# A retention layer and a gated feed-forward on one core: slot 5 transposed by DMA, two slots loaded by the hardware queue, a new order

## The chip, the cores and the metric

The kernel runs on one core of a Trainium2 chip. Its engines are TensorE (PE, its weight loads shown apart as PEld), VectorE (DVE), ScalarE (ACT), GpSimd (POOL) and SyncE (SP), which work through their own instruction queues and wait for each other by semaphores. Sixteen DMA engines move data; a transfer is issued either by POOL (in software) or by SP (in hardware). The metric is the device time of one execution in microseconds, the median of several runs.

## The reference

Inputs are q, k and v of shape (4, 8, 768, 64) (batch, head, time, head width), w_in (512, 2048) and w_out (2048, 512), all float32. What is computed:

```python
gamma = 1.0 - 2.0 ** (-5.0 - np.arange(H))
scale = 1.0 / np.sqrt(D)
for t in range(S):
    state = gamma * state + einsum('bhd,bhe->bhde', k[:, :, t], v[:, :, t])
    y[:, :, t] = scale * einsum('bhd,bhde->bhe', q[:, :, t], state)
x = y.transpose(0, 2, 1, 3).reshape(B * S, H * D)      # 3072 tokens of 512
h = x @ w_in
g = h * cos(h)
return g @ w_out
```

## The kernel before

**Slots.** Time is cut into six chunks of 128, batches are taken in two pairs, and one chunk of one pair is a slot: twelve slots, in the order 0, 6, 1, 2, 3, 4, 5, 7, ... of `ORDER`. In a slot the recurrence becomes matrix products: scores k times q, masked to the past, times v, plus q times the state of earlier chunks. q is multiplied by a rising power of gamma and k or v by a falling one ("conversions", `conv_q`, `conv_k`, `conv_v`, to bfloat16). q and k must also be transposed, so that the head width lies on the partitions.

**Transposes.** Slots 0 to 5 are transposed on TensorE against an identity (`t_mm`, L364), into a PSUM bank that ACT or DVE copies to `qkt` (`t_copy`). From slot `DMA_T` = 6 on, SP issues a DMA transpose of the converted q and one of k (`dma_t`, L353).

**Blocks.** The products of a slot with 64-row operands, its scores (L392), masked products (L483), state products (L497, L511), are put out in an order for the four quarters of TensorE's array (`y_block`, `quarters`). From slot 4 on a slot's block also holds the scores of the next slot. `second(p, x, b, u)` says which half of the chunk's keys counts as the later one: a product of the later half needs only 64 of 128 columns. In slots from `SWAP` = 8 on, the halves of k and v are loaded in swapped order for half of the heads and batches, so that the two column halves of the array have as many columns each; below that one has 128 and the other 64.

**Feed-forward.** Two slots are a group of 512 tokens. The first product (`f_mm`, L593; `h_mm`, L614, for the half group of one slot) has 16 blocks of w_in; ACT takes the cosine (L601), DVE multiplies (L605, L622), and the second product (`o_mm`, L638) has four rows of tokens times four quarters of w_out. ACT copies a row out and SP stores it.

**The order of the work.** All up to slot 5's block, groups 0 and 1, and the second product of group 0 is laid out by a planner when the program is written: `Plan` holds operations with engines, a cost, what they come after and a rank. `run` walks through time and gives every free engine the ready operation of the lowest rank; then they are written in the order of their starts, so each engine's queue is fixed. `SHIFT` adds to ranks by name and `ON` fixes an engine. For transfers `Plan.run` keeps one time `self.dma`, at which the transfers so far are through; `rate` and `lag` say how long one takes. What follows is a plain loop (groups 2 to 6), in which first and second products alternate and blocks, conversions, transposes (`conv`) and loads (`load(nc.sync, ...)`) stand at fixed places.

**Loads.** Five buffers each hold q, k and v as loaded (`PRE`). The first q is loaded by SP. All else in the planned part comes through POOL, in the order of `LOADS`: q, k, v of the slots, w_in in pieces, w_out in quarters o0 to o3, last v5, q6, k6, v6, q7, k7, v7. A load of 512 KB in POOL's queue holds POOL for some 1.2 us. Slot 8 is loaded by SP (`l8`, with "ks" and "vs": swapped halves, six DMAs each) after slot 7's transposes; later slots in the loop. The transposes of slots 6 and 7 wait for k7 (`ld["k", 7, 0]`).

**Names of the operations** that the text uses: q6, k6, v6 are loads; cq, ck, cv with slot and batch are conversions; t50, t51 slot 5's transposes on TensorE, eq and ek the copies; dt60 and dt61 the DMA transposes of q and k of slot 6; m the masks.

Of the kernel before, what the change touches and what calls it, by code (L numbers as in the profile page):

```python
# [28 lines left out]
class Plan:  # L29
# [16 lines left out]
    def add(self, engines, cost, fn, after=(), rank=0.0, take=(), give=(), mode=None,  # L46
            spare=0, mb=0.0, rate=0.0, lag=0.0, name=""):
        op = dict(engines=engines, cost=cost, fn=fn, after=[a for a in after if a], rank=rank,
                  take=take, give=give, mode=mode, spare=spare, mb=mb, rate=rate, lag=lag,
                  n=len(self.ops), start=None, done=None, free=None, name=name)  # L50
        self.ops.append(op)
        return op
# [12 lines left out]
    def run(self, start, cold_until=0.0, look=0.0, fill=None, hold=""):  # L65
# [4 lines left out]
        mode = [None]  # L70
        left = list(self.ops)
        t = 0.0
        while left:
            nxt = []
            for e in "SPADE":
# [6 lines left out]
                for op in left:  # L82
                    if e not in op["engines"]:
                        continue
                    r = self.ready(op)
# [27 lines left out]
                if e in hold and best:  # L113
                    c = best[1]["cost"]
# [14 lines left out]
                op = best[1]  # L129
# [14 lines left out]
                if op["mb"]:  # L144
                    self.dma = max(self.dma, t + busy + 1.6) + op["mb"] / op["rate"] + op["lag"]
                    op.update(done=self.dma + 0.9, lat=0.0)
# [21 lines left out]
SHIFT = {"ml010": 25.5, "mulf0.2": -74.7, "f0.3": 0.3, "cosf0.2": -11.6, "cosf0.3": -2.2, "mulf0.3": -4.9, "f0.2": 2.8, "m011": -20.0, "mulh1.4": -20.5, "m000": 82.7, "cosf0.5": -41.6, "ck21": 45.1, "a31": -124.5, "m100": 2.2, "f0.5": 23.0, "a5": -2.5, "v0": -97.2, "ms110": 6.4, "ml110": -41.8, "cosf0.4": -0.9, "f0.4": -9.8, "mulf0.5": 16.9, "eq51": 13.1, "m110": 64.4, "t20": -21.1, "k5": -46.0, "mulf0.8": 31.6, "yc21": -50.4, "f0.6": 2.1, "f0.7": 55.3, "ek10": -92.1, "w0b": -22.2, "a21": -34.2, "h1.0": 81.4, "cosh2.2": 3.0, "m501": 38.5, "yc30": -23.3, "ml011": -27.8, "mulf0.15": 5.8, "sc5": 79.1, "m201": -81.3, "mulh2.2": -18.0, "oc1": -45.8, "mulf0.14": -66.8, "cq31": -32.2, "mulf0.9": -47.9, "mulf0.6": 5.7, "cosf0.7": -27.8, "a30": -8.1, "cosf0.6": -7.2, "h0.2": -12.1, "eq21": -4.6, "cq51": 3.2, "cq41": 38.6, "f0.14": 23.8, "ek20": -13.4, "yc50": 39.8, "cv51": 23.4, "ek51": 88.5, "mulh2.10": 23.3, "cq70": 8.6, "f0.10": -46.0, "mulf0.13": 1.5, "h1.6": 5.9, "ml100": 20.1, "f0.15": 60.8, "o2.1": -8.1, "h3.10": 31.9, "t51": 14.8, "h3.0": -7.1, "h3.14": 28.8, "cq00": -2.7, "m601": 4.7, "h1.4": 1.8, "eq11": 37.0, "cosf0.12": -60.7, "v6": -26.4, "m400": 17.7, "mulh3.12": 67.0, "w2": 49.4, "sw": -53.6, "cv10": -0.0, "rv00": 14.5, "mulh2.8": 4.5, "ek50": 72.2, "cosf0.11": 2.4, "m101": -34.4, "h2.2": 1.1, "q2": -22.9, "q5": -59.7, "cosh3.14": 19.9, "y3": 19.8, "t40": 30.7, "o2": -0.8, "mulh3.4": -0.3, "cq40": -13.2, "mulh0.2": -29.3, "y5": -35.7, "mulh3.14": -25.5, "h2.12": -50.9, "oc0": -94.2, "a10": 39.9, "ek11": -35.3, "h0.6": 6.9, "eq40": -6.2, "h2.6": 58.1, "rv10": -9.1, "dt71": -1.3, "cosh3.8": -31.0, "cosh0.2": 18.8, "cv70": -67.6, "o3.1": -13.8, "cq60": -11.1, "ck60": 71.1, "m511": 10.9, "sc4": -15.9, "o1.3": -16.8, "m510": 4.5, "k4": 12.5, "h0.4": -9.2, "cq71": 3.6, "mulh3.2": 58.9, "cosh1.2": -26.7, "mulh3.6": -1.4, "cv61": 13.7, "o2.2": -9.8, "q6": -7.4, "o0.2": -7.5, "mulh2.4": 44.5, "mulh2.6": 22.6, "mulh3.10": 16.6, "v5": -53.7, "cq61": 27.8, "o1.1": -27.2, "ck61": 0.2, "m200": -10.8, "cosf0.9": 6.3, "cosh0.4": 11.6, "q4": 78.9, "cosh3.6": -6.8, "h1.2": -87.9, "tq01": 1.8, "oc3": -74.8, "mulh0.0": -16.9, "eq01": 11.2, "t21": 6.2, "ck41": 29.7, "cosh3.4": 9.3, "oc2": 8.6, "m211": 23.9, "cq01": -56.9, "w0a": 17.8, "o1.0": -7.7, "yc01": 2.2, "k7": 54.8, "yc51": -0.7, "cosf0.13": -14.9, "cosh2.10": -36.4, "yc00": 7.1, "cosh1.4": -13.4, "ek00": -8.7, "m611": -13.9, "tk10": -101.4, "mulh0.4": -40.7, "mulf0.10": 15.2, "m600": -35.2, "a00": -17.4, "cosh2.0": -5.5, "m301": 18.6, "rv11": -50.0, "sc0": -52.0, "ek01": -31.6, "cv01": 13.3, "ek21": -3.2, "cosf0.10": 7.2, "v7": -2.1, "ek40": 18.1, "t31": 22.7, "mulh1.6": 0.2, "eq30": -9.4, "y4": 19.2, "tk11": 1.9, "ek31": -26.9, "w3b": 23.5, "cosh2.12": -0.2, "cosh0.6": 4.7, "cosh2.8": -4.4, "cosh3.2": 25.8, "cv60": 2.7, "cosh2.4": -14.4, "v4": -1.1, "mulh2.12": 36.6, "dt61": -8.8, "eq41": -12.5, "mulf0.11": 31.8, "ek41": -0.8, "eq50": 9.1, "a11": -23.9, "yc10": 9.3, "o0.3": 0.3, "dt60": -3.3, "o3.3": 50.5, "mulh2.14": -42.3, "m610": -12.1, "f0.11": -0.6, "s0": 3.1, "cv11": 38.9, "h3.8": -17.4, "yc40": 14.3, "m410": -8.4, "h2.8": -4.0, "m300": 15.8, "o0": -14.6, "cv31": -27.4, "rv01": 0.6, "cosf0.14": 2.4, "cosh2.6": 11.7, "cv50": -6.8, "m010": -1.2, "ms011": -12.0, "f0.13": -5.2, "l8": 5.1, "ck70": 3.2, "t41": 1.0, "o1.2": -2.3, "cv71": 0.5, "tq11": 31.2, "h2.4": -3.6, "mulh0.6": 8.8, "t50": 7.1, "ck31": 42.7, "yc20": -52.3, "m001": -4.7, "y01": 62.0, "y2": 15.3, "f0.12": 20.5, "ms111": 2.0, "mulh1.2": -13.9, "cosh3.10": -49.0, "ck51": -9.0, "h0.0": -0.1, "eq31": 1.4, "eq20": -5.1, "q7": 1.5, "cosh3.0": 6.2, "cosh3.12": 1.5, "cv40": 2.3, "y11": 3.6, "o1": -24.4, "cv00": -1.4, "sc2": -3.2, "m411": 18.0, "m210": -8.1, "v3": 0.0, "eq10": 1.1, "tk01": 22.8, "yc41": -25.6, "cq21": -1.8, "f0.9": -31.4}  # L168
ON = {"cv70": "P", "cv00": "D", "cv30": "D", "cv31": "D", "cv60": "D", "cv11": "D", "cv10": "P", "rv01": "D", "sc5": "D", "rv11": "A", "yc20": "D", "sc3": "D", "eq40": "DA", "eq50": "A", "rv00": "A", "yc00": "D", "yc31": "DA", "ek51": "D", "ek11": "DA", "sc4": "D", "ek20": "A", "cv61": "P", "eq01": "DA", "cv51": "D", "ek41": "D", "eq41": "A", "cv20": "P", "yc01": "DA", "eq20": "A", "eq30": "DA", "ek50": "D", "ek00": "D", "sc2": "DA", "yc50": "DA", "yc40": "A", "yc21": "A", "cq21": "D", "ek40": "DA", "cv01": "D", "cv71": "P", "cv21": "P", "ek21": "DA", "cv41": "P", "cq20": "D", "ek10": "DA", "yc30": "A", "ek01": "D"}
# [4 lines left out]
def kernel(  # L174
# [11 lines left out]
    C = 128  # L186
# [10 lines left out]
    DMA_T = 6  # L197

    ORDER = [0, NC] + [x for x in range(1, NP) if x != NC]
    SWAP = 8  # L200
# [71 lines left out]

    SRC = {"q": (qf, q), "k": (kf, k), "v": (vf, v)}

    def load(eng, p, names):
# [4 lines left out]
        for n in names.split():  # L280
            t, src = SRC[n[0].lower()]
            if len(n) == 1:
                t = (qb(p) if n == "Q" else kb(p)) if n in "QK" else t[p % PRE]
                eng.dma_start(  # L284
# [3 lines left out]
            elif n[1] == "s":  # L288
                fl = t[p % PRE].rearrange("p b h d -> p (b h) d")
                for x in range(2):  # L290
                    for lo, n4, th in ((0, 4, x), (4, 8, 1 - x), (12, 4, x)):
                        eng.dma_start(
# [708 lines left out]
```

## Time and profile before

| what | us |
|---|---|
| median of three runs | 208.79 (208.3 to 209.35) |
| span of the profiled execution, first to last instruction | 206.6 |
| TensorE busy in it | 201.9 |
| ACT, DVE, POOL busy | 115.1, 112.9, 75.2 |

The profile gives the span of its execution and no other time of it, so its own time is the span; 208.79 less 206.6, 2.19 us, stands for what lies around it. How to read it: a profile is one execution; the page gives busy times, the span in 40 slices, and the chain of work that ended last. A timeline's line is start, length, engine, line of the kernel and operation, with what is written <- what is read. Lengths of pipelined products overlap, so a stretch of TensorE is read from the start of one line to the start of the next.

### The profile page before, as it was taken

To read this page: it belongs to the slowest core of one execution; us is meant where nothing else is said; L and a number is where in the kernel's file an instruction comes from. 1 tells how busy PE (TensorE), PEld (TensorE's weight loads), DVE (VectorE), ACT (ScalarE), POOL (GpSimd) and SP (SyncE) were. 2 spreads that over 40 slices of the span, in tenths; PEclk is the share of its full clock that TensorE was granted. 3 is DMA by queue.
4 is the path that set the end of the run, shared out by engine and by line. 5 is a ranking of instruction groups with operands and counts; after the bars stand their busy time and mean duration, and the time that the engine had idled before them with its cause. 6 is when DMAs were issued, how large, how long until landed. Compare 5 with 4: busy or idle time off the path is not lost.

```text
span 206.6 us, 5235 instructions
## 1 busy us (share of the span) xinstructions
PE 201.9 (98%) x2179; PEld 108.9 (53%) x2179; DVE 112.9 (55%) x194; ACT 115.1 (56%) x193; POOL 75.2 (36%) x79
## 2 busy tenths in 40 slices
PE   7999999999999999999999999999999999999994
PEld 2547665868945545445445445445444444444442
DVE  5477899776787548338438438448442444444000
ACT  7566794859965357547547546554555553554120
POOL 8899989799985003305206105200000000000000
PEclk9999999999999999999999999999999999999999
DMA  6999999999999865886876975501101101110212
GB/s 117 172 264 201 304 242 322 252 333 278 341 332 190 199 156 150 206 210 155 190 183 157 144 198 147 156 0 56 53 1 51 51 3 51 51 51 0 105 52 102
DMA packets 59656, 32.15 MB, mean 156 GB/s; under 512 B 48752, under 2 KB 54128, under 8 KB 59632
## 3 DMA queue, kind: packets, MB, share of 16 engines
q0 software_dynamic: 15408, 15.47, 34.6%
q1 hardware_dynamic: 44080, 16.28, 31.7%
q8 instruction: 17, 0.28, 0.6%
q10 hardware_dynamic: 144, 0.07, 0.1%
q14 instruction: 7, 0.06, 0.1%
HBM read 27.26 MB, written 6.29 MB: 162 GB/s over the span
## 4 chain that ended last, share of the span: by engine, by line
PE 93%; DMA 4%; POOL 1%; issue 0%; DVE 0%; POOLq 0%; DVEq 0%
PE bank L638 39%; PE bank L593 30%; PE bank L614 10%; DMA kx<-in_k_dram 4%; PE bank L392 2%; PE bank L483 2%; PE bank L364 2%; PE bank L658 2%; PE st_ps L511 2%; PE bank L667 2%; PE bank L497 1%; POOL ks L284 1%; PE bank L434 1%; POOL qs L284 1%; PE bank L402 0%
## 5 line engine op out<-in xcount | busy, mean ns | idle before, releaser
L601 ACT ACTIVATE cosb<-bank,halfpi 128x512 bf16<-128x512 f32 x96 | 65.6, 689 | 54.1 <-PE bank L593 47.8
L638 PE MATMUL bank<-w_out_sb,gt 128*128 128x512 bf16 x368 | 91.0, 379 | 0.0
L605 DVE TENSOR_TENSOR gt<-bank,cosb 128x512 bf16<-128x512 f32 x72 | 49.1, 689 | 55.7 <-ACT cosb L601 55.7
L593 PE MATMUL bank<-xt,w_in_sb 128*128 128x512 bf16 x288 | 73.2, 379 | 0.0
L638 PEld LDWEIGHTS <-gt 128*128 128x128 bf16 x368 | 35.5, 98 | 42.3 <-DMA w_out_sb<-in_moe_w_out_dram 0.3
L593 PEld LDWEIGHTS <-w_in_sb 128*128 128x128 bf16 x288 | 27.5, 98 | 32.3
L327 POOL TENSOR_TENSOR qs<-qf,gq 128x512 bf16<-128x512 f32 x18 | 18.5, 1046 | 42.4 <-PE bank L483 32.0
L411 DVE TENSOR_TENSOR am<-bank,mask 128x512 bf16<-128x512 f32 x40 | 24.8, 681 | 3.5 <-PE bank L392 3.5
L316 ACT COPY ob<-bank 128x512 f32<-128x512 f32 (+1 forms) x24 | 14.0, 582 | 16.0 <-PE bank L638 13.9
L614 PE MATMUL bank<-xt,w_in_sb 128*128 128x256 bf16 x192 | 22.4, 273 | 0.0
L614 PEld LDWEIGHTS <-w_in_sb 128*128 128x128 bf16 x192 | 18.6, 98 | 3.3 <-DVE xt L318 0.3
L622 DVE TENSOR_TENSOR gt<-bank,cosb 128x512 bf16<-128x512 f32 x24 | 16.2, 689 | 5.6 <-ACT cosb L601 5.4
L316 ACT CAST xt<-bank 128x512 bf16<-128x512 f32 x21 | 11.4, 588 | 10.6 <-PE bank L483 10.5
L316 ACT CAST ks<-kf 128x512 bf16<-128x512 f32 x20 | 11.5, 623 | 1.9 <-DMA kf<-in_k_dram 1.9
L667 PE MATMUL bank<-zero 128*128 128x512 bf16 x35 | 11.2, 449 | 1.1 <-DVE halfpi L683 1.1
L483 PE MATMUL bank<-am,vs 64*64 64x128 bf16 (+1 forms) x320 | 10.3, 206 | 0.1
L334 POOL TENSOR_TENSOR vs<-vf,gk 128x512 bf16<-128x512 f32 x8 | 8.2, 1043 | 6.0 <-DMA vf<-in_v_dram 3.8
L284 POOL DMA_DIRECT2D vf<-in_v_dram x8 | 9.4, 1178 | 1.9 <-DVE vs L339 1.4
L339 POOL TENSOR_TENSOR vs<-vf,gk 128x512 bf16<-128x512 f32 x8 | 8.7, 1096 | 2.5 <-PE bank L483 1.3
L318 DVE CAST stb<-st_ps 128x512 bf16<-128x512 f32 x9 | 6.2, 689 | 3.4 <-PE st_ps L511 2.6
L483 PEld LDWEIGHTS <-vs 64*64 64x64 bf16 x320 | 7.8, 107 | 0.5 <-POOLq L531 0.2
L392 PE MATMUL bank<-qkt 64*64 64x128 bf16 (+1 forms) x320 | 7.9, 206 | 0.0
(66 smaller groups left out, 131.7 us busy)
## 6 DMA issues: line engine op xcount, KB each, us to landing
out_dram<-ob SPq DMA_DIRECT2D x23, 256.0 KB, 2.5
vf<-in_v_dram POOLq DMA_DIRECT2D x8, 512.0 KB, 11.7
qf<-in_q_dram POOLq DMA_DIRECT2D x6, 512.0 KB, 12.3
kf<-in_k_dram POOLq DMA_DIRECT2D x6, 512.0 KB, 12.1
w_out_sb<-in_moe_w_out_dram POOLq DMA_DIRECT2D x4, 512.0 KB, 14.1
qf<-in_q_dram SPq DMA_DIRECT2D x4, 512.0 KB, 4.8
w_in_sb<-in_moe_w_in_dram POOLq DMA_DIRECT2D x5, 256.0 KB, 8.5
kf<-in_k_dram SPq DMA_DIRECT2D x16, 64.0 KB, 3.1
```

What stands on the lines that cost most here:

```text
L284: eng.dma_start(out=t.rearrange("p b h d -> p (b h) d"), in_=src[ds(2 * bp, 2), :, ds(c * C, C), :].rearrange("b h t d -> t (b h) d"))
L316: nc.scalar.copy(out=out, in_=in_)
L327: ENG[e].tensor_tensor(out=qb(p)[:, b], in0=qf[p % PRE][:, b], in1=bc(gq, ORDER[p] % NC), op=ALU.mult)
L411: nc.vector.tensor_tensor(out=am[p % 2][b][u], in0=bank.rearrange("p (a t) -> p a t", a=HP), in1=(dec[:, b] if p < 2 else mask[second(p, 0 ...
L483: m = nc.tensor.matmul(held["yp", p][b][ts(j, 64), a, lo:], lhsT=vs[p % NB][ts(r, 64), b, h, :], rhs=am[p % 2][b][h // 4][ts(r, 64), h % 4 ...
L593: nc.tensor.matmul(bank, lhsT=w_in_sb[:, i, ts(f, 128)], rhs=xt[g % 2][:, i, :], start=(i == 0), stop=(i == KIN - 1))
L601: nc.scalar.activation(out=cb, in_=bank, func=AF.Sin, bias=halfpi)
L605: nc.vector.tensor_tensor(out=gt[g % 2][:, f, :], in0=bank, in1=cb, op=ALU.mult)
L614: nc.tensor.matmul(bank[:, ts(e, 256)], lhsT=w_in_sb[:, i, ts(f + e, 128)], rhs=xt[g % 2][:, i, ts(hf, 256)], start=(i == 0 and e == 0), s ...
L622: nc.vector.tensor_tensor(out=gt[g % 2][:, f : f + 2, ts(hf, 256)], in0=bank.rearrange("p (f t) -> p f t", f=2), in1=cb.rearrange("p (f t) ...
L638: nc.tensor.matmul(bank, lhsT=gt[g % 2][:, f, ts(j, 128)], rhs=w_out_sb[:, f, :], start=(f == 0), stop=(f == KOUT - 1))
L667: nc.tensor.matmul(bank[:, : 256 * n].rearrange("p (n t) -> p n t", n=n), lhsT=zero[:, :128], rhs=zero.unsqueeze(1).to_broadcast([128, n, ...
```

## The change

- `DMA_T` goes from 6 to 5: slot 5's q and k are transposed by two DMAs from SP (dt50, dt51), not by TensorE; t50, t51 and their four copies are gone.
- q, k and v of slots 6 and 7 leave `LOADS` and become `HWL`, issued by SP. In front of them SP has a `nop` that waits for the landing of o3, the quarter of w_out that is the last but one in `LOADS` (`gate`). The transposes wait for the gate to be issued, no longer for k7.
- `SWAP` goes from 8 to 6: k and v of slots 6 and 7 are loaded with swapped halves too. A swapped load has four DMAs, two of 128 partitions and two of 64, where it had six of 64; that holds for slot 8 and later ones as well.
- In the planner's account: a start of 6.78 for `self.dma`, other rates and lags, an own latency `first` per transfer, and the transposes take their turn in `self.dma`.
- `SHIFT` and `ON` are new. Of the ranks: a load on SP has 10 * (slot - 1), a transpose 10 * slot, slot 8's load 80; to that `SHIFT` adds as below.

```diff
+SHIFT = {
...
+"q6": -10.8, "k6": -6.9, "v6": 134.6, "q7": 64.8, "k7": 54.2, "v7": 51.9,
...
+"dt50": 4.9, "dt51": -4.7,
...
+"dt60": -2.4, "dt61": -2.1,
...
+"dt70": -6.3, "dt71": -29.7, "sw": -54.1, "l8": 95.5,
...
-    DMA_T = 6
+    DMA_T = 5
+    HWF = 6
...
-    SWAP = 8
+    SWAP = 6
...
-                for x in range(2):
-                    for lo, n4, th in ((0, 4, x), (4, 8, 1 - x), (12, 4, x)):
-                        eng.dma_start(
-                            out=fl[ts(x, 64), ds(lo, n4), :],
...
+                for to, n, at, lo, m in ((0, C, 0, 0, 4), (0, C, 0, 12, 4),
+                                         (0, 64, 64, 4, 8), (64, 64, 0, 4, 8)):
+                    eng.dma_start(
+                        out=fl[ds(to, n), ds(lo, m), :],
+                        in_=src[ds(2 * bp, 2), :, ds(c * C + at, n), :]
+                        .rearrange("b h t d -> t (b h) d")[:, ds(lo, m), :])
...
-    LOADS = [... "o3", "v5", "q6", "k6", "v6", "q7", "k7", "v7"]
+    LOADS = [... "o3", "v5"]
+    HWL = ["q6", "k6", "v6", "q7", "k7", "v7"]
...
+    def gate(e):
+        x = LOADS[-2]
+        after(held["load", int(x[1:]), x[0]], nc.sync.nop(nofuse=True))
+
+    x = LOADS[-2]
+    go = add("S", 0.05, gate, [ld[("o", int(x[1])) if x[0] == "o" else (x[0], int(x[1:]), 0)]], 20,
+             name="gate")
+    prev = go
+    for x in HWL:
+        p = int(x[1:])
+        n = x[0] + ("s" if x[0] != "q" and p >= SWAP else "")
+        o = add("S", 0.55 if len(n) == 1 else 2.4, lambda e, p=p, n=n: load(nc.sync, p, n),
+                [("issued", prev)], 10 * (p - 1), mb=524288e-6, rate=285e-3, first=1.5, name=x)
...
-                T["dt", p, w] = add("S", (1.3, 4.6), lambda e, p=p, w=w: dma_t(p, w),
-                                    [T["c" + x, p, 0], T["c" + x, p, 1], ld["k", 7, 0]] + old, 10 * p,
-                                    name="dt%d%d" % (p, w))
+                T["dt", p, w] = add("S", 1.3, lambda e, p=p, w=w: dma_t(p, w),
+                                    [T["c" + x, p, 0], T["c" + x, p, 1], ("issued", go)] + old, 10 * p,
+                                    mb=262144e-6, rate=230e-3, first=-0.4, name="dt%d%d" % (p, w))
```

## The prediction

> **What bounds the kernel now.** I read the page first (span, busy times, the span in slices), then the chain of waits of TensorE, then its timeline between 10 and 72 us, then the timelines of SP and POOL for the transfers that the change moves.
>
> The page, parts 1 and 2 (each digit is a fortieth of the span, 5.17 us):
>
> ```profile
> span 206.6 us, 5235 instructions
> ...
> PE 201.9 (98%) x2179; PEld 108.9 (53%) x2179; DVE 112.9 (55%) x194; ACT 115.1 (56%) x193; POOL 75.2 (36%) x79
> ...
> PE   7999999999999999999999999999999999999994
> ...
> POOL 8899989799985003305206105200000000000000
> ...
> DMA  6999999999999865886876975501101101110212
> ```
>
> TensorE is busy in every slice; POOL and the DMA engines are full only in the first 65 us. The same in two stages, cut where the first real product starts and where the written-out loop starts:
>
> ```profile
> 15.75:69.62 53.87, 53.85 (x862) 37.86 (x861) 41.51 (x70) 37.67 (x64) 44.98 (x43) 1.00 1.12 276
> 69.62:203.00 133.38, 133.25 (x1199) 63.90 (x1198) 61.66 (x94) 66.76 (x107) 16.35 (x16) 1.00 0.41 106
> ```
>
> The second column is the length, the third TensorE's busy time: 53.85 of 53.87 us. From 15.75 us on TensorE waits for nothing, and the granted clock (1.00) is full. So the end moves by the TensorE work that goes, minus each new wait of TensorE; work saved on other engines is worth nothing by itself.
>
> TensorE's timeline: start, length, line, operation.
>
> ```profile
> 14.23 1.69 PE L667 MATMUL bank<-zero 128*128 128x512 bf16 x7
> 15.75 1.04 PE L614 MATMUL bank<-xt,w_in_sb 128*128 128x256 bf16 x8
> 16.72 0.64 PE L434 MATMUL bank<-am,gt 128*64 128x128 bf16 x16
> 17.29 0.39 PE L667 MATMUL bank<-zero 128*128 128x512 bf16 x1
> ...
> 55.38 0.39 PE L364 MATMUL bank<-ident,qs 128*128 128x128 bf16 x4
> 55.61 0.39 PE L364 MATMUL bank<-ident,ks 128*128 128x128 bf16 x4
> 55.83 0.39 PE L364 MATMUL bank<-ident,qs 128*128 128x128 bf16 x4
> 56.05 0.39 PE L364 MATMUL bank<-ident,ks 128*128 128x128 bf16 x4
> 56.28 1.04 PE L614 MATMUL bank<-xt,w_in_sb 128*128 128x256 bf16 x8
> ...
> 63.72 4.49 PE L638 MATMUL bank<-w_out_sb,gt 128*128 128x512 bf16 x20
> ```
>
> L667 multiplies zeros to fill time; only one such instruction lies behind 15.75. The L364 lines are slot 5's sixteen transposes; lengths overlap in the pipeline, so cost is read from start to start: 55.38 to 56.28 is 0.90 (slots 2 and 3 show 0.89). SP's queue, where the change puts work:
>
> ```profile
> 62.56 1.33 SPq L353 DMA_TRANSPOSE qkt<-ks  x1
> 64.07 3.37 SPq L353 DMA_TRANSPOSE qkt<-qs  x2
> 67.55 1.24 SPq L353 DMA_TRANSPOSE qkt<-ks  x1
> 68.89 0.54 SPq L650 DMA_DIRECT2D out_dram<-ob  x1
> 69.53 0.39 SPq L284 DMA_DIRECT2D qf<-in_q_dram  x1
> 70.02 5.87 SPq L292 DMA_DIRECT2D kf<-in_k_dram  x6
> ```
>
> SP does nothing between 8.4 and 59.6 us; its transposes take 1.23 to 1.34 us each to issue (one 1.97), and landed 2.8 to 4.4 us after the start of issue.
>
> **The change, part by part.** The sum is made against the profiled execution, whose span is 206.6; its own launch-to-end time is not given, so what lies around the span is taken as 208.79 - 206.6 = 2.19 us, the same before and after.
>
> *Slot 5's transposes.* Sixteen TensorE transposes go: -0.90 us on the path, since TensorE is never idle there. Four evictions of them go too, two of 0.59 on ACT and two of 0.42 on DVE: nothing, both engines had spare time (ACT 37.7 and DVE 41.5 of the 53.9 us). Two DMA transposes come on SP, 2 x 1.3 us of issue and 256 KB each; in 64 to 66 us transposes moved 224 GB/s, so about 1.2 us each on the DMA engines. Their landing is needed at slot 4's block, which starts at 62.23 and carries slot 5's scores; 0.9 us earlier after the change, 61.3.
>
> [...] The timeline gives 0.056 us for one 128x128 transpose on TensorE in a stream and 1.3 us of issue for eight by DMA. [...]
>
> *Swapped halves for slots 6 and 7.* The scores and masked products of a slot are the same number of columns, but spread evenly over the quarters of the array. The blocks of the state (start to next product) last 1.49 us at 62.23, 68.14 and 77.50 (both slots unswapped), 1.40 at 92.91 (next slot swapped) and 1.32, 1.37, 1.32 at 108.23, 123.46 and 138.75 (both swapped). After: slot 5's block 1.40, slot 6's 1.32, slot 7's 1.37. Saved: 0.09 + 0.17 + 0.03 = 0.29 us, all on TensorE.
>
> *Six loads leave POOL.* 6 x 1.18 = 7.1 us of issue go between 42.98 and 53.11; POOL is not the bound, so nothing by itself. But slot 5's q conversions, behind them at 53.11 to 55.16, can run when q5 has landed (issued at 35.20, 13.5 us to landing: 48.7), so they are ready when the gate opens.
>
> *The gate and SP's queue.* The nop waits for w_out's last quarter, issued at 37.52 with 15.2 us to landing: 52.7. In front of it SP has nothing else to do. Behind it stand all of SP's loads, transposes and output stores. By the ranks of the diff (base plus shift) the order is q6 39.2, k6 43.1, dt51 45.3, dt50 54.9, dt60 57.6, dt61 57.9; v6 has 184.6 but goes whenever SP has nothing readier, and q7, k7, v7 go behind it. From SP's rows: q 0.5, the first piece of a k load 1.5 to 1.8 and the others 0.62, so k6 in four pieces 3.7. Gate 52.7, q6 to 53.2, k6 to 56.9, slot 5's two transposes to 59.5, landed by 58.2 + 2.8 = 61.0 (needed 61.3). k6 lands 2.5 to 3.1 us behind its last issue at 56.3: 58.8 to 59.4; ACT's two conversions of 0.57: 60.0 to 60.6. If v6 has started by then (four pieces, 2.5 us), SP is free at 62.0; the two transposes of slot 6 are issued at 62.0 and 63.3 and land at 66.1, with the longest row of 4.4 at 67.7. They are needed inside slot 5's block, whose first such product stood 0.4 us behind its start: 68.14 + 0.4 - 0.9 = 67.6. So between -1.5 and +0.1 us of lateness by these rows; 0 is taken, as the two longest rows of before stood in a queue of four transposes.
>
> Both ends for the unknown part. Best: no wait. Worst: slot 8's load in the trace, also on SP and in 256-byte pieces, took from 69.53 to the landing of its last k piece 8.2 us (last issue 75.25, 2.5 more), and slot 5's transposes could go first (2.6): k6 at 52.7 + 2.6 + 8.2 = 63.5, conversions 64.7, second transpose issued at 66.0, landed at 70.4: 2.8 us late. A gain from the queue alone is excluded, as TensorE does not wait there now.
>
> *The DMA engines.* While POOL's loads ran they moved 342 GB/s (55 to 60 us); SP's loads in 256-byte pieces moved 253 to 286 (87 to 89, 72 to 73 us). Six slots' parts of 0.524 MB are 9.2 us by the one and 11 to 12.4 by the other: 1.8 to 3.2 us more, plus 2.4 for slot 5's transposes. v7 landed at 63.4 (issued 51.95, 11.4 to landing); now some 69. It is hidden: slot 7 is needed in slot 6's block at 77.50, and its transposes, 1.3 of issue and 2.8 to landing behind its k, come 4 us before that. If that cover is gone, each us of lateness is a us. [...]
>
> *Slot 8's load* moves back, as SP issues some 24 us from the gate to it (six transposes 7.8, four swapped loads at 2.5 to 3.7, two q, stores): 77 instead of 69.5. But it has nine pieces instead of thirteen, 6.7 us instead of 10.3: to 84 instead of 79.9. Slot 8's transposes, issued at 82.18 now, go to some 85 to 87 and land by 90; slot 7's block wants them at 92.91 - 1.2 = 91.7. Nothing.
>
> *The new ranks and engines.* Before 15.75 TensorE waits for q, k, v and the first columns of w_in, whose loads keep their order. One zero product of 0.22 us behind 15.75 could go, and the first product could start at most 0.25 us earlier (the evictions in front of it end at 15.2): bound -0.47. The other bound is as much idle time as another order leaves; TensorE has none now, the order is fixed when written, and the nearest row is the 0.22: +0.22 and more. I take 0.
>
> Sum: -0.90 - 0.29 + 0 = -1.19 us; 206.6 becomes 205.4, and 208.79 becomes 207.6.
>
> **The rivals.**
> *The queue of SP comes too late (slower).* Place: slot 5's block waits for slot 6's second transpose. For it: one queue carries now what two carried, and after the gate 8.2 us of issue (q6, k6, four transposes) must be done before that block. Against it: the four transposes of before also waited, for the landing of k7 (issued 50.76, 11.0 to landing: 61.8), and that wait is gone. It decides from 2.2 us late on (1.19 + 0.5% of 208.79): landing after 69.8. At the worst bound of 2.8 us it gives 207.6 + 2.8 = 210.4.
> *The freed time comes back as idle time.* Slot 4's block, the four masks of slot 5 (2.48 us on DVE, 64.56 to 67.04) and slot 5's block are a chain; 63.72 to 68.14 lies between the two blocks, filled with five units of L638. If slot 5's transposes land a us late, that chain moves and there is too little to fill it with: 0.4 to 1.5 us of idle time, 208.0 to 209.1. For it: 61.0 against 61.3 is close. Against it: L638 units can stand ahead of the block instead.
> *The order gains more.* The 0.47 us of the start: 207.1.
> *The change does not do what it says*: if the gate opened only with POOL's last load (54.2 for v5), SP's work would start 1.5 us later and the second rival holds.
>
> **How the numbers follow.** The forecast 0.52, the late queue 0.23, idle time 0.19, the better start 0.06. Runs of before spread over 208.3 to 209.35, and 0.5% is 1.04 us, about what a measurement of this kernel can tell from no change; 207.6 is just beyond it (207.75), so of the 0.52 I put 0.41 on faster and 0.11 within. The late queue counts 0.22 slower and 0.01 within, idle time 0.17 within and 0.02 slower. Faster 0.41 + 0.06 = 0.47; within 0.11 + 0.01 + 0.17 = 0.29; slower 0.24. Range: from the better start with 0.2 of spread, 206.9, to the worst bound, 210.4.
>
> **What would show it.** Right: no L364 for slot 5 and 16 transposes fewer; blocks of 1.40, 1.32 and 1.37; transposes of slot 5 issued by SP near 57; TensorE's busy time still as long as the stage; the loop's first product (71.36) about 1.1 us earlier. Wrong: idle time of TensorE put down to qkt or to masks near 61 to 68, or zero products behind 18 us; a first product later than 15.75.

## The result and the profile after

The changed kernel takes 215.16 us (median, 213.75 to 215.43) against 208.74 for the kernel before, measured beside it: a ratio of 1.0292 with an interval of 1.0255 to 1.0329. It is 6.4 us slower by the medians and 6.1 by the ratio, where 1.2 us faster was forecast, and it lies above the range of 206.9 to 210.4. The profiled execution took 214.93 us with a span of 213.1, so 1.8 us lie around the span; the 2.19 us that the prediction took for that joined a median to the span of another execution.

The page of the kernel after, parts 1 and 2, a digit for 5.33 us:

```profile
span 213.1 us, 5194 instructions
...
PE 202.8 (95%) x2166; PEld 108.2 (51%) x2166; DVE 111.9 (52%) x191; ACT 114.8 (54%) x192; POOL 68.2 (32%) x73
...
PE   7999998999999886999999999999999999999991
...
PEclk9999999999999997999999999999999999999999
DMA  7999999999989999899595893411101101111121
```

TensorE, busy in every slice before, has a gap in slices 14 to 16 (69 to 85 us), and the granted clock has a dent at the end of it. The DMA engines stay at 8 tenths or more up to slice 19, 101 us; before it was up to slice 14, 72 us. To size this, cut both spans at three marks: the first real product, slot 5's block, and a product behind slot 6's block. The columns are start:end, length, TensorE's busy time with its instructions, the other engines, the granted clock, the DMA engines' share and GB/s. The kernel before:

```profile
15.75:68.14 52.39, 52.37 (x751) 36.47 (x750) 41.23 (x69) 37.67 (x64) 44.98 (x43) 1.00 1.12 277
68.14:80.73 12.59, 12.59 (x270) 7.03 (x270) 7.79 (x13) 6.59 (x12) 2.04 (x2) 1.00 0.75 171
80.73:203.00 122.27, 122.14 (x1042) 58.25 (x1041) 54.15 (x82) 60.16 (x96) 14.30 (x14) 1.00 0.39 101
```

The kernel after:

```profile
15.22:68.32 53.10, 52.53 (x738) 35.98 (x737) 40.27 (x66) 36.09 (x60) 33.77 (x33) 1.00 1.10 249
68.32:86.08 17.76, 13.80 (x266) 6.97 (x266) 9.03 (x15) 6.67 (x12) 5.29 (x6) 0.90 0.88 212
86.08:208.50 122.42, 122.29 (x1046) 58.36 (x1045) 52.90 (x80) 60.73 (x97) 15.08 (x15) 1.00 0.40 103
```

The second stage is 5.2 us longer (12.59 to 17.76), though one unit of L638, 0.86 us, has moved from it to the first (64 such products there, 60 before). From its end to the start of the last products it is the same, 119.2 and 119.1 us (80.73 to 199.91, 86.08 to 205.19). The waits of TensorE in the kernel after:

```profile
PE bank L392 <- DMA qkt<-ks: 3.8, 2, 2.7
PE bank L667 <- DVE halfpi L683: 1.1, 1, 1.1
PE bank L638 <- DMA w_out_sb<-in_moe_w_out_dram: 0.5, 1, 0.5
```

The first line is new: scores that wait for a transposed k, once in slot 5's block (for slot 6's k) and once in slot 6's block (for slot 7's). The second was there before. TensorE's timeline at the longer wait:

```profile
78.90 0.22 PE L497 MATMUL bank<-qkt,stb 64*64 64x128 bf16 x2
81.81 0.24 PE L392 MATMUL bank<-qkt 64*64 64x64 bf16 x2 [2.68 <-DMA qkt<-ks]
...
82.77 1.89 PE L593 MATMUL bank<-xt,w_in_sb 128*128 128x512 bf16 x4
84.45 1.78 PE L638 MATMUL bank<-w_out_sb,gt 128*128 128x512 bf16 x4
86.08 1.03 PE L593 MATMUL bank<-xt,w_in_sb 128*128 128x512 bf16 x4
86.94 0.81 PE L638 MATMUL bank<-w_out_sb,gt 128*128 128x512 bf16 x3
```

After 2.68 idle microseconds the next two units take 1.68 and 1.62 us from start to start instead of 0.86. The clock record shows 0.5 from 82.56 to 85.97, for 3.41 us.

The account, by starts of TensorE's work (us against the kernel before):

| place | us |
|---|---|
| first real product at 15.22, not 15.75 | -0.53 |
| first stage: sixteen transposes -0.90, one unit of L638 more +0.86, w_out's first quarter awaited (eight L593 products take 2.44, not 1.74) +0.70, rest | +0.71 |
| second stage, one unit less: -0.86 | |
| ... slot 5's block 2.77, not 1.49 | +1.28 |
| ... the L638 unit behind it 1.24, not 0.86 (wait for xt) | +0.38 |
| ... slot 6's block 4.32, not 1.49 | +2.83 |
| ... two units at half clock, 3.31, not 1.74 | +1.57 |
| second stage in all | +5.17 |
| third stage | -0.07 |
| last product's end to the end of the span 4.30, not 3.03 | +1.27 |
| sum of start, stages and tail (the spans, 213.1 and 206.6, differ by as much) | +6.55 |

Of the 6.55 us, some 6.1 are the two late blocks, the unit behind the first and the clock behind the second, and 1.27 are the tail, which the last section comes back to; the rest takes 0.8 off. The 0.53 us of an earlier start was no gain: the stream caught up with w_out's first quarter (landed at 32.78, before at 32.55) and waited for it.

What came so late was SP's queue. SP's timeline after the gate:

```profile
52.39 0.37 SPq L286 DMA_DIRECT2D qf<-in_q_dram  x1
52.81 3.54 SPq L294 DMA_DIRECT2D kf<-in_k_dram  x4
56.52 1.34 SPq L355 DMA_TRANSPOSE qkt<-ks  x1
57.98 1.24 SPq L355 DMA_TRANSPOSE qkt<-qs  x1
...
59.94 3.12 SPq L294 DMA_DIRECT2D vf<-in_v_dram  x4
63.17 1.28 SPq L355 DMA_TRANSPOSE qkt<-qs  x1
64.63 1.23 SPq L355 DMA_TRANSPOSE qkt<-ks  x1
...
67.06 2.20 SPq L286 DMA_DIRECT2D qf<-in_q_dram  x1
69.35 4.14 SPq L294 DMA_DIRECT2D kf<-in_k_dram  x4
73.59 2.90 SPq L294 DMA_DIRECT2D vf<-in_v_dram  x4
...
77.34 1.34 SPq L355 DMA_TRANSPOSE qkt<-qs  x1
78.79 1.24 SPq L355 DMA_TRANSPOSE qkt<-ks  x1
```

Slot 6's k is transposed from 64.63 and lands at 70.04; slot 7's k is loaded until 76.40 (landing), transposed from 78.79 and lands at 81.76, where TensorE resumes. Between these rows stand four output stores (left out above). What the DMA engines did meanwhile, in the kernel before:

```profile
53.00:57.00 4.00, 4.00 (x47) 3.69 (x45) 3.64 (x7) 3.63 (x7) 3.98 (x5) 1.00 1.03 341
57.00:61.00 4.00, 4.00 (x50) 1.98 (x49) 3.62 (x7) 2.43 (x5) 3.04 (x4) 1.00 1.03 347
```

and in the kernel after:

```profile
53.00:57.00 4.00, 4.00 (x39) 3.58 (x38) 3.47 (x6) 3.12 (x6) 1.56 (x2) 1.00 0.93 212
57.00:61.00 4.00, 4.00 (x55) 2.43 (x53) 3.18 (x6) 3.31 (x6) 1.80 (x2) 1.00 1.03 236
61.00:65.00 4.00, 4.00 (x125) 2.42 (x124) 2.14 (x4) 1.48 (x3) 0.00 (x0) 1.00 0.77 174
65.00:69.00 4.00, 4.00 (x54) 1.89 (x52) 3.70 (x6) 1.34 (x3) 1.04 (x1) 1.00 1.06 144
69.00:73.00 4.00, 2.73 (x85) 1.63 (x83) 2.10 (x4) 1.09 (x3) 0.00 (x0) 1.00 0.96 258
73.00:77.00 4.00, 4.00 (x20) 1.82 (x19) 0.98 (x2) 0.50 (x1) 2.04 (x2) 1.00 0.82 184
```

The engines were busy for a share of 1.03 before and of 0.77 to 1.06 after (the last column but one), yet they moved 341 to 347 GB/s of POOL's loads before and 144 to 258 of SP's mix after, on average 201.

### The profile page after: what moved, and what is told of

Its sections match the earlier page's. It is cut to its first block, busy times and chain, and to the rows that moved or that the text cites. A ratio compares the mean times of both kernels' runs of the same rounds, so it can differ in the third digit from the quotient of the medians.

```text
span 213.1 us, 5194 instructions
## 1 busy us (share of the span) xinstructions
PE 202.8 (95%) x2166; PEld 108.2 (51%) x2166; DVE 111.9 (52%) x191; ACT 114.8 (54%) x192; POOL 68.2 (32%) x73
## 4 chain that ended last, share of the span: by engine, by line
PE 74%; DMA 12%; POOL 5%; SPq 3%; ACT 2%; issue 1%; DVE 0%; ACTq 0%; POOLq 0%; DVEq 0%
PE bank L638 35%; PE bank L593 25%; PE bank L614 7%; DMA w_out_sb<-in_moe_w_out_dram 6%; DMA vf<-in_v_dram 3%; PE bank L392 2%; PE bank L483 2%; DMA kf<-in_k_dram 2%; PE bank L658 2%; SPq L294 2%; DMA qkt<-ks 1%; PE st_ps L511 1%; SPq L286 1%; PE bank L497 1%; PE bank L364 1%
## 5 line engine op out<-in xcount | busy, mean ns | idle before, releaser
L638 PE MATMUL bank<-w_out_sb,gt 128*128 128x512 bf16 x368 | 92.0, 382 | 0.5 <-DMA w_out_sb<-in_moe_w_out_dram 0.5
L593 PE MATMUL bank<-xt,w_in_sb 128*128 128x512 bf16 x288 | 74.0, 383 | 0.2 <-ACT xt L318 0.2
L638 PEld LDWEIGHTS <-gt 128*128 128x128 bf16 x368 | 35.7, 98 | 43.5 <-issue 1.1
L593 PEld LDWEIGHTS <-w_in_sb 128*128 128x128 bf16 x288 | 27.7, 98 | 33.3 <-issue 1.7
L318 ACT CAST xt<-bank 128x512 bf16<-128x512 f32 x21 | 11.4, 588 | 11.9 <-PE bank L483 11.7
L336 POOL TENSOR_TENSOR vs<-vf,gk 128x512 bf16<-128x512 f32 x11 | 11.3, 1043 | 15.7 <-DVE am L411 7.1
L392 PEld LDWEIGHTS <-qkt 64*64 64x64 bf16 x320 | 6.3, 108 | 5.0 <-DMA qkt<-ks 4.0
L320 DVE CAST stb<-st_ps 128x512 bf16<-128x512 f32 x7 | 4.8, 690 | 6.4 <-PE st_ps L511 6.4
L286 POOL DMA_DIRECT2D vf<-in_v_dram x6 | 7.1, 1192 | 1.3 <-DVE gt L622 0.8
```

What stands on the lines that cost most here:

```text
L318: nc.scalar.copy(out=out, in_=in_)
L336: ENG[e].tensor_tensor(out=vb(p)[:, b].rearrange("p (u x) d -> p u x d", u=2), in0=vf[p % PRE][:, b].rearrange("p (u x) d -> p u x d", u=2 ...
L392: return nc.tensor.matmul(ap[b][ts(x, 64), a, lo:], lhsT=kt(p % NB, b, h)[:, ts(x, 64)], rhs=qt(p % NB, b, h)[:, lo:], tile_position=(64 * ...
L593: nc.tensor.matmul(bank, lhsT=w_in_sb[:, i, ts(f, 128)], rhs=xt[g % 2][:, i, :], start=(i == 0), stop=(i == KIN - 1))
L638: nc.tensor.matmul(bank, lhsT=gt[g % 2][:, f, ts(j, 128)], rhs=w_out_sb[:, f, :], start=(f == 0), stop=(f == KOUT - 1))
```

## The experiments

The expectations call the theories by letters; A, B and C stood at the start, B2 and D came after the first runs. A: SP's issue time sets the lateness. B: the DMA engines are too slow for the 256-byte pieces; as B2: what SP's one queue can move sets it, as loads, transposes and stores go through it one behind the other. C: the new order of the planned part costs the time by itself. D: transposes starve on the DMA engines while POOL's loads run, which would be why the change took those loads off POOL. Ratios are to the kernel before on the same chip; the kernel after has 1.0292.

### Slot 7's loads through POOL

```diff
-lambda e, p=p, n=n: load(nc.sync, p, n)
+lambda e, p=p, n=n: load(nc.gpsimd if p == 7 else nc.sync, p, n)
```

> The changed kernel, but q, k and v of slot 7 are issued by POOL at the same place of the written order; all other queues are the same. Theory A (SP's one queue: everything behind the gate is issued one after the other, so slot 7's loads start at 67.1 and its second transpose at 78.8): slot 7's loads start some 5 us earlier, its transposes are issued by 72, slot 6's block has no wait for them (-3.0 us) and the two half-rate products behind it (-1.6 us) go: span 213.1 - 4.6 = 208.5, time about 210.4. The wait in slot 5's block (1.4 us) stays. Theory B (the DMA engines are too slow for the 256-byte pieces): the bytes are the same, so at least 2 of the 3.0 us stay: time over 214. Theory C (the new order of the engines' work loses the time): all as in the changed kernel, 215.

213.78 us, ratio 1.0219 (1.0163 to 1.0275). Slot 7's k lands at 68.4 instead of 76.40 and the wait in slot 6's block is gone (1.31 us). But slot 5's block lasts 5.35 us: the issue of slot 6's first transpose takes 4.31 us while POOL's loads run, the second is issued at 68.64 and lands at 71.73. The wait moved to the block before; neither A's 210.4 nor the wait in slot 6's block that B keeps came.

### Loads in one piece, halves not swapped

```diff
-    SWAP = 6
+    SWAP = 8
-0.55 if len(n) == 1 else 2.4
+0.55 if x[0] == "q" else 2.4
```

(The second line only keeps the planner's account as it was.)

> The changed kernel without the swapped halves in slots 6 and 7, so that each k and v load is one instruction instead of four, with the planner's costs kept. Theory A: SP saves 2.5 to 3 us at each of four loads, slot 7's second transpose comes some 8 to 10 us earlier, slot 6's second transpose some 3 to 5 us earlier; no wait in either block, and blocks of 1.49, 1.49 and 1.40 us: span 213.1 - 4.6 - 1.7 + 0.3 = 207.1, time about 209. Theory B: the same bytes in the same 256-byte pieces go through the same queue, the waits stay: 214 to 215. Theory C: 215.

211.6 us, ratio 1.0131 (1.0094 to 1.0169). There are twelve DMA instructions less, yet slot 7's k lands at 75.92, 0.5 us earlier than in the kernel after, and slot 6's block lasts 5.27 us in the profile. SP's timeline of this run shows why:

```profile
53.80 3.54 SPq L355 DMA_TRANSPOSE qkt<-ks  x1
...
59.91 4.04 SPq L355 DMA_TRANSPOSE qkt<-qs  x1
...
68.78 1.44 SPq L286 DMA_DIRECT2D kf<-in_k_dram  x1
...
72.44 3.29 SPq L650 DMA_DIRECT2D out_dram<-ob  x1
```

Issues of 1.3 and 0.5 us now take 3.3 to 4.0: what SP saves by fewer instructions it spends in longer ones; no view shows what holds them. That speaks against A for slot 7. For slot 6 A holds in part: its second transpose is issued 0.5 us earlier (64.11), lands at 66.98, and slot 5's block has no wait (1.49). The gain against the kernel after is 3.4 us by the ratios. The profiled run is the longest of four, and the other three kept the full clock (1.00, after 0.98 to 0.99), so a part of the gain is the clock's.

### Slot 5 back on TensorE

```diff
-    DMA_T = 5
+    DMA_T = 6
```

> The changed kernel with slot 5's transposes back on TensorE (the planner orders anew). Theory A: SP's queue is 2.6 us shorter in front of slot 7's loads, so slot 7's second transpose lands near 79 and slot 6's block waits under 0.5 us, the half-rate products go, and 0.9 us of transposes come back on TensorE: time about 211.5, faster than the changed kernel though TensorE has more to do. Theory B: 0.5 MB less on the DMA engines, a gain of at most 2 us less the 0.9: about 214. Theory C: no gain, 215 to 216.

210.33 us, ratio 1.0065 (1.0043 to 1.0087): with 0.90 us more work for TensorE, 4.7 us faster than the kernel after by the ratios. SP has less in front of it, and by the planner's ranks slot 7's q and k now go ahead of slot 6's transposes:

```profile
60.26 0.56 SPq L286 DMA_DIRECT2D qf<-in_q_dram  x1
60.92 4.81 SPq L294 DMA_DIRECT2D kf<-in_k_dram  x4
65.84 1.35 SPq L355 DMA_TRANSPOSE qkt<-qs  x1
```

Slot 7's k lands at 67.99; slot 6's block has no wait (1.32), and slot 5's has 1.4 us (2.84 in all). The gain is larger than A (211.5) or B (214) expected, and as two transposes less take both issue time and bytes off SP's queue, this run does not tell A from B. The bytes ahead of slot 7's k and the time to its landing, over five runs:

| kernel | from the gate to the landing of slot 7's k | what the queue carried | GB/s |
|---|---|---|---|
| after | 24.0 us | five loads, four transposes, three stores: 4.46 MB | 186 |
| in one piece | 23.8 us | the same, 4.46 MB | 187 |
| slot 5 on TensorE | 15.1 us | five loads, one store: 2.88 MB | 191 |
| two v loads out (below) | 19.7 us | four loads, four transposes, three stores: 3.93 MB | 200 |
| slot 7's k ahead of slot 6's v (below) | 17.7 us | four loads, two transposes, one store: 2.88 MB | 163 |

(A load is 0.524 MB, a transpose or a store 0.262.) More bytes take longer, but not by bytes alone: the same 2.88 MB took 15.1 us without a transpose and 17.7 with two.

### Zero products in front of slot 6's block

```diff
             if p < NP and r == 3:
+                if p == 6:
+                    for i in range(12):
+                        idle_mm("E", 2)
                 block(p)
```

> The changed kernel with twelve zero products (2.6 us) put in front of slot 6's block, so that TensorE is not idle while slot 7's transpose is awaited. If the half-rate products behind that wait (1.6 us) come from the idle time, through the granted clock, they go and nothing else changes: the clock record shows full rate throughout, span 211.5, time about 213.5. If they come from something else at that place, the time stays at 215; if the zeros add to the wait, 217.

213.1 us, ratio 1.0196 (1.0175 to 1.0217). The granted clock stays at 1.00 throughout, and the units behind the block are back at 0.86 us:

```profile
80.51 1.67 PE L667 MATMUL bank<-zero 128*128 128x512 bf16 x7 [0.22 <-DVE gt L605]
83.43 1.04 PE L593 MATMUL bank<-xt,w_in_sb 128*128 128x512 bf16 x4
84.30 0.59 PE L638 MATMUL bank<-w_out_sb,gt 128*128 128x512 bf16 x2
```

So the half clock comes from the idle time, not from the slot's operands. The two units end at 85.16 instead of 86.08: 1.57 us regained, 0.66 lost as the block ends later behind the zeros (83.43, not 82.77). Of the 2.0 us between the two spans this is 0.9; the other 1.1 are the tail, 3.20 us here, whose two lengths the last section shows.

### Loads back on POOL, transposes of slot 5 kept

```diff
-... "o3", "v5"]
-    HWL = ["q6", "k6", "v6", "q7", "k7", "v7"]
+... "o3", "v5", "q6", "k6", "v6", "q7", "k7", "v7"]
+    HWL = []
-    SWAP = 6
+    SWAP = 8
```

(The gate goes on waiting for o3.)

> The changed kernel with the loads of slots 6 and 7 back in POOL's list behind v5, in one piece and unswapped; slot 5 is still transposed by DMA behind the gate, and the planner orders anew. The first runs leave two theories. Theory B2 (throughput of SP's queue): what stands behind the gate on SP goes through one queue in order at some 250 MB per ms, and its 5 MB end at 76; POOL's queue moves 345 and would end them at 63.4 as before. Then there is no wait in the blocks of slots 5 and 6, and the time is 208.8 - 0.9 = 207.9. Theory D (slot 5's transposes are the trouble in whichever queue the loads are, because they share the DMA engines with them): slot 4's block, which needs slot 5's transposes at 62 to 63, waits 1 to 3 us: 209 to 211.

210.63 us, ratio 1.0060 (1.0026 to 1.0095). Slot 5's transposes, issued at 53.02 and 54.67, land 11.4 and 12.0 us later, at 64.47 and 66.72; POOL's loads end at 63.9. Slot 4's block is late by 0.7 us and slot 5's by 1.65. D is right that slot 4's block waits, if for less than the 1 to 3 us it named, and still this is 4.8 us faster than the kernel after: the planner, ordering anew, puts slot 4's block at 65.81, so that little of the late landing is waited for.

### The kernel before with slot 5's transposes by DMA alone

```diff
-    DMA_T = 6
+    DMA_T = 5
-T["c" + x, p, 1], ld["k", 7, 0]] + old
+T["c" + x, p, 1], ld["k", 7, 0] if p > 5 else ld["o", 3]] + old
```

> The kernel before with slot 5's transposes alone moved to DMA, issued by SP as soon as the conversions are done (some 55 us), beside POOL's loads that run until 63.4. The planner keeps the old ranks and loads. If transposes get their share of the engines (theory B2): landed by 60, no wait, 0.9 us off TensorE: 207.9. If they starve beside POOL's larger packets until the loads end at 63.4 (theory D): slot 4's block starts 2 to 3 us late, 210 to 211.

215.58 us, ratio 1.0295 (1.0241 to 1.0348): as slow as the whole change, and beyond the 210 to 211 that D named. The rows of the transposed tile between 52 and 56 us:

```profile
L353 SPq DMA_TRANSPOSE qkt<-ks x1: 1340/1340/1340, 52.7 to 52.7; - x1
L353 SPq DMA_TRANSPOSE qkt<-qs x1: 5725/5725/5725, 55.1 to 55.1; - x1
...
DMA to landing us min/median/max: 11.8/11.8/11.8
```

The transpose of k lands after 11.8 us and that of q takes 5.7 us to issue (its own landing is not in the record), where the four transposes of slots 6 and 7 in the kernel before took 1.23 to 1.97 us to issue and 2.8 to 4.4 to land. Slot 4's block comes at 61.88, lasts 5.00 us instead of 1.49, and the clock halves at 65.98. The packet records say how they starve: from 57 to 59 us POOL's queue sent 152 packets of 3.6 KB on average and SP's 145 of 256 bytes, from 59 to 61 us 169 and 167: 277 to 313 GB/s for the one, 19 to 21 for the other. The two queues sent about equal numbers of packets, and the one with the small packets got a fifteenth of the bytes; no run varied the size of the packets.

### The order alone

```diff
-    DMA_T = 5
+    DMA_T = 6
-    SWAP = 6
+    SWAP = 8
-    HWL = ["q6", "k6", "v6", "q7", "k7", "v7"]
+    HWL = []
-("issued", go)] + old
+("issued", go), ld["k", 7, 0]] + old
```

(The six loads stand in `LOADS` again, as two experiments above; ranks and engines are those of the kernel after.)

> The changed kernel's ranks, engines and planner figures alone: slot 5 on TensorE, no swapped halves in slots 6 and 7, all loads by POOL and the wait for k7, as in the kernel before. Theories B2 and D: the order itself is harmless, 208.8, at most 0.7 us more for the wait for w_out's first quarter that the changed kernel shows at 32.1. Theory C (the new order loses by itself): 211 or more.

209.81 us in ten runs, ratio 1.0037 (1.0016 to 1.0059): 0.3 to 1.2 us slower than before. TensorE waits 1.0 us for w_in, and slot 5's block lasts 2.27. C is worth 0.8 us here, with ranks that were drawn for other operations; it doesn't explain 6.4. The 1.0 us wait for w_in is not in the kernel after, so this is not the order's price there.

### The gate opened by slot 5's q

```diff
-        x = LOADS[-2]
+        x = "q5"
```

> The changed kernel with the gate opened by q5's landing (48.3) instead of o3's (52.3); every queue's order is the same. Theory A (SP's issue time): SP's chain starts 4 us earlier, slot 7's second transpose is issued at 75, the 3.0 us wait and the half-rate products go: about 210. Theory B2: between 48 and 54 the DMA engines are already full with POOL's loads, so the queue gains at most 1 to 2 us, and v5 and o3 come later by as much: 213 to 215.

214.82 us, ratio 1.0241 (1.0177 to 1.0305), not told apart from the kernel after. The gate opens at 48.96 instead of 52.39, but the first piece of slot 6's k then takes 3.76 us to issue beside POOL's loads, slot 5's first transpose is issued at 56.10 (56.52), and slot 7's k lands at 76.55 (76.40). In the profiled run, the longest of the four, slot 5's block has no wait (1.39 us) and slot 6's lasts 6.07. Opening the gate earlier, at a time when the DMA engines' share is already 1.01 (48.96 to 52.39 us in the kernel after), gains nothing, as B2 said and A did not.

### Four loads left out

```diff
-load(nc.sync, p, n)
+load(nc.sync, p, n) if n in ("q", "ks") and p == 6 else None
```

> The changed kernel with v6, q7, k7 and v7 left out (the buffers' older contents are used, so the result is not the reference's); all engines' queues but SP's are the same. Theory B2 (what SP's queue can move): 2.1 of some 5 MB behind the gate are gone, slot 6's transposes stand right behind slot 5's, slot 7's follow, and no block waits. Then the forecast's own terms show: -0.90 for the transposes, -0.29 for the swapped halves, some 0.2 for the wait at w_out's first quarter: span near 205.8, time near 208.0. If the blocks still wait, the loads are not the cause and transposes or stores are: 211 or more.

208.76 us in ten runs, ratio 0.9982 (0.9960 to 1.0005). The waits of TensorE:

```profile
PE bank L667 <- DVE halfpi L683: 1.1, 1, 1.1
PE bank L593 <- ACT xt L318: 0.2, 1, 0.2
```

No wait for a transpose is left; the blocks of slots 4 to 7 last 1.49, 1.40, 1.32 and 1.34 us. The last products start at 198.81, 1.10 us earlier than in the kernel before. The tail, 4.02 us instead of 3.03, gives 1.0 of that back.

### Slot 7's k ahead of slot 6's v

```diff
-    HWL = ["q6", "k6", "v6", "q7", "k7", "v7"]
+    HWL = ["q6", "k6", "q7", "k7", "v6", "v7"]
```

> The changed kernel with q7 and k7 issued before v6 on SP; the bytes are the same. Theory B2: the queue is in order, so slot 7's transposes come where v6 and v7 were less in front of them, 3 us earlier or more, and the wait of slot 6's block (3.0) and its half-rate products (1.6) go or shrink; but q7 and k7 (1.05 MB) now stand in front of slot 6's transposes where v6 (0.52 MB) stood, at 250 MB per ms 2 us more wait in slot 5's block: about 212 to 213. If only the sum of bytes counted and not their place, 215 as in the changed kernel.

213.31 us, ratio 1.0181 (1.0132 to 1.0231). Slot 7's k lands at 70.15 and slot 6's block has no wait (1.32), but slot 6's second transpose, now behind 1.05 MB of slot 7 instead of 0.52 MB of v6, is issued at 67.94 and lands at 72.53: slot 5's block lasts 5.22 us, and the clock halves at 73.23. As with POOL, what is put first only picks the block that waits, at this load of the queue.

### Loads held until slot 6's transposes have landed

A version of my own: all loads by POOL in one piece, in the order q6, k6, q7, k7, v6, v7, those behind k6 held by a `nop`; the ranks drawn anew.

```diff
+    def held_load(p, n):
+        if p == 7 and n == "q":
+            w = nc.gpsimd.nop(nofuse=True)
+            for x in range(2):
+                after(held["dt", p - 1, x], w)
+        load(nc.gpsimd, p, n)
```

> A version drawn from the runs: all loads by POOL in one piece (no swapped halves in slots 6 and 7), slot 5 transposed by DMA, and POOL holds back q7, k7, v6 and v7 until slot 6's transposes have landed, so that transposes do not run beside POOL's loads for long; ranks drawn anew for it. Slot 5's transposes, issued at 52.7, get the engines when k6 has landed (57.4) and land by 60 to 61; slot 6's by 65; slot 7's near 75. If the shares of the engines are what the theory says, no block waits: 208.8 - 0.9 = 207.9, at worst 209. If the transposes are slow even with the engines to themselves, slot 4's or 5's block waits 1 us or more: 209 to 211.

209.99 us in ten runs, ratio 1.0041 (1.0015 to 1.0066). Slot 5's transposes land at 58.35 and 59.25, slot 6's at 60.77 and 64.12, and neither block waits (1.49 each). But slot 7's q is issued only at 65.16, its k lands at 74.18, the second transpose at 79.79, and slot 6's block lasts 3.75 us. It spares the transposes of slots 5 and 6 and pays at slot 6's block; no version that does all the work is faster than the kernel before.

### Two v loads left out

```diff
-load(nc.sync, p, n)
+load(nc.sync, p, n) if n != "vs" else None
```

> The changed kernel with v6 and v7 left out (older contents of the buffers are used, so the result is not the reference's): half of what the run without four loads left out, the other queues the same. Theory B2: 0.52 MB less in front of slot 6's transposes and of k7 (2.1 to 2.6 us), another 0.52 MB less in front of slot 7's transposes: the wait in slot 5's block (1.4) goes, that in slot 6's block (3.0) shrinks to under 0.5, no half-rate products: time 208.8 to 209.5. If a single hold of the DMA engines, as that of 1.8 us at 67.2 in the changed kernel, makes the lateness and the bytes do not, 1 to 2 us of wait stay in slot 6's block: 211 or more.

208.41 us in ten runs, ratio 0.9972 (0.9946 to 0.9998). Of the transposes, the loads they need and the stores nothing is removed, only 1.05 MB of v (0.52 of it ahead of slot 7's k). The k of slot 7 lands at 71.88, its transpose at 76.63, the blocks last 1.49, 1.40, 1.32 and 1.32, and the last products start at 198.89, 1.02 us earlier than before. With the two v loads out the whole loss is gone, so it comes from what stands in SP's queue. How much of it is bytes and how much issue is not separated: slot 7's k came 4.5 us sooner for 0.52 MB less, which at the rates of the table is 2.6 to 3.2 us, and leaving slot 6's v out takes 3.1 us of SP's issue away too. Against A as the whole cause stand the run in one piece and the earlier gate. The rival of a single hold of the engines falls: by the packet records no packet begins for 1.0 us at 61.5 and for 1.5 us at 72.2 in this run (0.85 us at 67.2 in the kernel after), and no block waits.

## Why the prediction was wrong

**The step that failed** is the one headed "The DMA engines". It said of slot 7 "v7 landed at 63.4 (issued 51.95, 11.4 to landing); now some 69. It is hidden". v7 landed at 78.80, k7 at 76.40, the second transpose of slot 7 at 81.76, where about 78.9 was wanted. Two terms were mis-sized. The rate, 253 to 286 GB/s, was read in short stretches in which SP's loads ran by themselves; in a queue with transposes and stores, counted from the gate to the landing, it is 163 to 200. And the bytes left out slot 6's transposes and the stores, 1.3 MB ahead of k7. With these 4.46 MB the prediction's own 270 GB/s would have put k7 at 52.4 + 16.5 = 68.9, still in time; with the measured rate it is 24.0 us, so the rate is the larger error, 7.5 us. The step also contradicted another: for slot 8's load SP was counted 24 us of issue from the gate, to 77; the same count ends with slot 7's second transpose, issued at about 75.7 and landed at 78.5 by the prediction's own 1.3 and 2.8 us, where its block was forecast to want it at 77.50 + 0.4 - 1.2 = 76.7; it was not carried over. What makes the gap to POOL's 342 GB/s is not shown: no run varied the piece size alone.

**Slot 6's transposes**, "between -1.5 and +0.1 us of lateness by these rows; 0 is taken": issued at 63.17 and 64.63 (forecast 62.0 and 63.3), the second landed after 5.4 us, not 2.8 to 4.4, at 70.04. Slot 5's block lasted 1.37 us longer than the forecast 1.40. The worst end named there, 70.4, was nearly reached.

**The late queue as a rival** had the right mechanism, one queue for what two carried, and the wrong place and price. It looked at slot 5's block alone, at most 2.8 us. The larger wait stood a block later, 3.0 us, and 1.57 us more came from something that no rival had: the clock after an idle stretch.

**The other rival**, idle time because slot 5's transposes come a little late, didn't happen: they landed at 59.90 and 60.81 (forecast 61.0), and slot 4's block lasted 1.50.

**What was right.** The -0.90 and -0.29 us are there: without waits, blocks of 1.40, 1.32 and 1.32 to 1.34 (forecast 1.40, 1.32, 1.37) and last products 1.02 to 1.10 us earlier, for 1.19. By the ratios of those two runs 0.4 to 0.6 us are left of it, and the interval of the first includes no change; the tail takes 1.0 in one trace and 0.2 in the other. The gate opened at 52.39 (52.7), k6 landed at 58.88 (58.8 to 59.4). Slot 8's load was issued from 80.12 to 87.61, later than the 77 to 84 forecast, but its transposes landed by 93.08 and slot 7's block, at 98.26, did not wait for them, as said.

**The new order** was taken as 0 with a gain of up to 0.47 at the start. The start came 0.53 us earlier and was lost again in 0.70 us at w_out, some 0.2 us in all in the kernel after; the run of the order alone, with another wait, gave 0.8.

**How it adds up.** The run of the order alone cost 0.8 us; slot 5's transposes with POOL's loads 1.3; SP's loads without slot 5's transposes 1.4; both together 6.1 (by the ratios, each in the new order; slot 5's transposes alone in the old order cost 6.2; slot 4's block stands at 61.88 there and at 65.81 in the new). The parts do not add up. Both draw on the slack of one queue, and taking 1.05 MB out of it was enough for no block to wait; less was not tried.

Not settled: how much of the lateness is issue and how much bytes, what holds the mix at some 200 GB/s while the DMA engines are busy 77 to 106% of the time, and why the tail has two lengths.

## What to carry to other kernels

Before a transfer is called hidden, list all that its queue carries ahead of it, in order and in bytes (transposes, stores and later loads included), and divide by a rate measured in that mix; a rate of one kind in a short stretch was too good here (253 to 286 GB/s, where the mix moved 163 to 200). Moving work to a queue where it is not on the critical path still spends that queue's slack, and two uses that cost 1.3 and 1.4 us alone cost 6.1 together here. A wait can cost more than its length: behind the idle 2.68 us here the clock was 0.5 for 3.41 us, which cost 1.57 us on top, so price a late transfer with that on top.

## What was not expected of the hardware

**The clock fell behind a wait of TensorE, for whole steps of 3.41 us.** It was 0.5 for 3.41 us in every trace with a wait of 2.7 to 3.4 us (after, slot 7's loads on POOL, loads in one piece, k ahead of v, the kernel before with slot 5 by DMA), for 6.83 us with one of 3.9 (the earlier gate), and stayed full with one of 2.0 (held loads) and of 1.2 (slot 5 on TensorE). The stretches at full clock are multiples of 3.41 us too: 78.51 and 126.29 us in the kernel after are 23 and 37 of them, 201.39 in the kernel before 59. In these traces the clock fell with a wait of 2.7 us and not with one of 2.0; no run varied the length of a wait alone, and what decides between them is not shown.

**A transpose by DMA** landed after 2.7 to 5.4 us in the kernel after, and slot 5's after 11.4 to 12.0 beside POOL's loads (11.4 and 12.0 with the loads back on POOL, 11.8 in the kernel before with slot 5 by DMA).

**The last store has two lengths.** ACT's last issue in the kernel before:

```profile
203.98 0.37 ACTq L662 DMA_DIRECT2D out_dram<-ob  x1
```

and in the kernel after:

```profile
209.27 1.46 ACTq L662 DMA_DIRECT2D out_dram<-ob  x1
```

Nothing of the change lies near it. It took 1.2 to 1.5 us in five of the fourteen traces (after, loads in one piece, k ahead of v, the earlier gate, four loads out) and 0.37 in the others. In the five it starts 0.1 us behind the end of SP's last store issue, in the others 0.4. That is a coincidence in time; no run tried the cause.
